# Transposing q and k by DMA instead of on TensorE for five of eight batches of an attention and mixer kernel

## The chip, the cores and the metric

The kernel runs on one core of a Trainium2 chip. The metric is the device time of one execution in microseconds (us), given as the median of several runs. One further execution was profiled; its span is the time from its first to its last instruction.

## The reference, cut to what matters

Eight batches are computed. In each, eight heads of attention over 576 positions with 64 features run under a mask: heads 0 to 3 ("plain") see the last 32 positions, heads 4 to 7 ("dilated") every fourth of the last 128. The result goes through an MLP mixer, first over tokens, then over channels.

```python
scores = scale * np.matmul(q, k.transpose(0, 1, 3, 2))      # q, k, v: (8, 8, 576, 64) float32
mask_plain = (rel >= 0) & (rel < window)                    # window 32
mask_dil = (rel >= 0) & (rel < window * dilation) & (rel % dilation == 0)   # dilation 4
...
attn = attn / (np.sum(attn, axis=-1, keepdims=True) + 1e-09)
return np.matmul(attn, v).astype(np.float32)
...
h = np.maximum(xt @ w_tok1, 0.0) @ w_tok2                   # xt: (8, 512, 576)
u = x + h.transpose(0, 2, 1)
h2 = np.maximum(u @ w_ch1, 0.0) @ w_ch2                     # 512 -> 1536 -> 512
return (u + h2).astype(np.float32)
```

## The kernel before, in words

All matrix work is float16 with float32 sums. The work is a software pipeline over the batches. In stage b (the loop at line 762) the channel MLP of batch b runs as the main thread (`gen_main`, line 517): 24 groups of four `gp` matmuls (line 529), then the `yp` matmuls (lines 546 and 566), whose sums plus `u` are stored by SyncE (SP). Steps of later batches are woven in: the attention values (`av`, line 396 and on), token mixing (`h1p`, `up`, line 438) and the transposes of the mixed rows (`tpu`, from line 467) of batch b+1, and the casts, transposes and scores of q and k of batch b+2. The loads of batch b+3 follow. Stages 1 to 5 thus hold the scores of batches 3 to 7.

The order is written out by hand: `interleave` (line 575) sorts the steps by a planned time, a number that counts about as us of TensorE work from the start of the stage, and issues each as soon as the planned time of the main thread has reached it. The scheduler is manual, so every engine executes its instructions in the order in which they are issued there, and an instruction that waits holds up everything behind it on its engine. This holds for SP too, whose only work is to issue DMAs. A DMA of SP also waits until the DMA eight places before it in this order has landed.

What happens to q and k of a batch, for each of four pairs of heads (`hp`; 0 and 1 plain, 2 and 3 dilated):

- SP loads them as float32 (`load_qk`, `load_tail`, lines 183 to 192). Partition m holds positions 4m to 4m+3, so that rows are long; the last 64 positions of both (the tails) are a tile of their own.
- GpSimd (POOL) casts them to float16 tiles `c_q`, `c_k`, `c_t` (line 103, planned from 2.0 in steps of 0.6).
- `transposes` (line 264) turns each pair around on TensorE: four 128x128 transposes for q and four for k (line 270), one for the tails (line 288 or 290), each a weight load and a matmul against the identity into PSUM. ScalarE (ACT, line 101; pairs 0 and 1) and VectorE (DVE, line 103; pairs 2 and 3) copy q from PSUM to `qz`, in two halves of 64 partitions, since the other half of each head's slot stays zero; DVE copies k to `kt` (line 275).
- `scores_plain` and `scores_dil` (lines 329 and 359) multiply `kt` and `qz` (line 320) into two PSUM banks in turn, and ACT takes the exponential into `attp` and `attd`. For batches from 2 on POOL multiplies these by the mask (line 113).

`kt` and `qz` lie in natural order of positions for the plain pairs; for the dilated pairs `qz` lies by residue of the position modulo 4, and the scores read every fourth column of `kt`. The mixed rows of batch b+1 are u = `up` + `xn`, added on DVE (line 445), one block of 128 rows after the other (s = 4, 0, 1, 2, 3); all of them are read by the `tpu` transposes.

## Time and profile before

| | |
|---|---|
| median of 3 runs | 310.79 us (310.61 to 312.88) |
| span of the profiled execution | 310.9 us, 8148 instructions |
| busy: PE, PE weight loads | 298.8 us, 268.3 us |
| busy: DVE, ACT, POOL | 168.4, 152.9, 148.4 us |
| DMA packets | 67606, 43.24 MB |
| stages 1 to 5 (from 73.00, 111.37, 145.48, 182.03 and 216.14 to 252.69 us) | 38.37, 34.11, 36.55, 34.11, 36.55 us |

The time of the profiled execution outside its span is not given apart; its span lies 0.1 us above the median of the runs, so sums made on the span carry over to the median as they are. PE is TensorE's matmuls, PEld its weight loads, which overlap with matmuls. A row of a timeline has the start in us, the duration in us, the engine, the line, the operation and its tiles (out<-in), and behind a bracket how long the engine stood idle before it and what ended that. The duration of a matmul runs from its start to its modelled end and overlaps with the next; what one costs is the distance between starts. A row of groups ends with the busy us and the mean ns of one.

### The profile page before, as it was taken

How to read it: one execution, taken by the hardware profiler on the slowest of the kernel's cores; microseconds unless marked ns; L12 is line 12 of the kernel's file. 1: busy time of each engine (PE TensorE's matmuls, PEld its weight loads, DVE VectorE, ACT ScalarE, POOL GpSimd, SP SyncE). 2: the span in 40 equal slices, each digit the busy share in tenths (PEclk: the TensorE clock that was granted, in tenths of full speed). 3: DMA queues.
4: the chain of work that ended last, by engine and by line, in shares of the span. 5: the costliest groups of instructions: out<-in, count | busy, mean ns of one | idle time of the engine just before them, and what ended most of it. 6: DMA issues, size and time to landing. Idle time of an engine off the chain costs nothing.

```text
span 310.9 us, 8148 instructions
## 1 busy us (share of the span) xinstructions
PE 298.8 (96%) x3292; PEld 268.3 (86%) x3292; DVE 168.4 (54%) x372; ACT 152.9 (49%) x349; POOL 148.4 (48%) x214
## 2 busy tenths in 40 slices
PE   5789999999999999999999999999999999999995
PEld 2677999988988999899987999899987999899884
DVE  5686448756656554655744655555745646523221
ACT  2664436286645635375545635475555635413500
POOL 7872065429970897029930897019940770000000
PEclk9999999999999999999999999999999999999999
DMA  7999999847995529821495129711001130021023
GB/s 216 267 211 180 235 268 291 242 136 215 275 293 126 170 86 289 172 70 60 121 261 136 64 92 306 153 50 57 33 2 27 45 101 3 0 70 67 2 69 103
DMA packets 67606, 43.24 MB, mean 139 GB/s; under 512 B 35920, under 2 KB 66512, under 8 KB 67568
## 3 DMA queue, kind: packets, MB, share of 16 engines
q1 hardware_dynamic: 63328, 37.63, 44.4%
q0 software_dynamic: 2640, 3.91, 7.1%
q10 hardware_dynamic: 1600, 1.18, 1.3%
q8 instruction: 26, 0.43, 0.6%
q14 instruction: 12, 0.10, 0.1%
HBM read 37.04 MB, written 9.44 MB: 149 GB/s over the span
## 4 chain that ended last, share of the span: by engine, by line
PE 91%; DVE 3%; ACT 2%; DMA 2%; issue 1%; ACTq 0%; POOLq 0%
PE gp L529 30%; PE yp L546 26%; PE h1p L426 4%; PE sc L320 4%; PE up L438 4%; PE yp L566 3%; PE tp_q L270 2%; PE tp_k L270 2%; DMA const<-consts 2%; PE sm L320 1%; PE tpu L475 1%; PE av L396 1%; PE h1p L424 1%; PE av L407 1%; PE sc L319 1%; PE tpu L467 1%
## 5 line engine op out<-in xcount | busy, mean ns | idle before, releaser
L529 PE MATMUL gp<-uT,w 128*128 128x288 f16 x768 | 109.9, 286 | 0.7 <-ACT uT L101 0.6
L546 PE MATMUL yp<-w,gt 128*128 128x256 f16 x756 | 93.8, 273 | 0.0
L107 ACT ACTIVATE gt<-gp 128x288 f16<-128x288 f32 x138 | 56.6, 410 | 72.1 <-PE gp L529 65.3
L529 PEld LDWEIGHTS <-w 128*128 128x128 f16 x768 | 83.1, 114 | 8.1 <-issue 1.2
L546 PEld LDWEIGHTS <-gt 128*128 128x128 f16 x768 | 76.0, 106 | 3.9
L113 POOL TENSOR_TENSOR attp<-attp,const 128x1280 f16<-128x1280 f16 (+1 forms) x24 | 35.8, 1515 | 77.8 <-ACT attp L349 67.0
L109 DVE TENSOR_SCALAR gt<-gp 128x288 f16<-128x288 f32 x54 | 24.6, 455 | 35.5 <-PE gp L529 33.9
L556 DVE TENSOR_TENSOR o<-yp,u 128x512 f32<-128x512 f32 x31 | 21.4, 690 | 34.4 <-PE yp L546 34.1
L113 POOL TENSOR_TENSOR attd<-attd,const 128x1024 f16<-128x1024 f16 (+1 forms) x24 | 32.8, 1394 | 0.0
L113 DVE TENSOR_TENSOR xn<-av,rec 128x320 f16<-128x320 f32 x64 | 31.5, 492 | 2.2
L320 PEld LDWEIGHTS <-kt 128*128 128x128 f16 x352 | 27.7, 104 | 3.6 <-DVE kt L275 1.4
L275 DVE COPY kt<-tp_k 128x512 f16<-128x512 f16 x32 | 21.8, 684 | 9.3 <-PE tp_k L270 9.3
L320 PE MATMUL sc<-qz,kt 128*128 128x128 f16 (+1 forms) x224 | 25.8, 228 | 1.0 <-ACT qz L101 0.7
L101 ACT COPY qz<-tp_q 64x576 f16<-64x576 f16 (+1 forms) x32 | 19.9, 621 | 6.1 <-PE tp_q L290 3.6
L340 ACT ACTIVATE attp<-sc 128x480 f16<-128x480 f32 x32 | 17.8, 573 | 9.5 <-PE sc L320 9.0
L445 DVE TENSOR_TENSOR u<-up,xn 128x512 f16<-128x512 f32 x26 | 17.9, 691 | 8.0 <-PE up L438 8.0
L103 POOL CAST c_q<-l_q 128x512 f16<-128x512 f32 x31 | 18.8, 609 | 5.7 <-DMA l_q<-in_q_dram 5.7
L369 ACT ACTIVATE attd<-sc 128x512 f16<-128x512 f32 x32 | 17.9, 596 | 5.8 <-PE sc L320 3.2
L103 POOL CAST c_k<-l_k 128x512 f16<-128x512 f32 x29 | 17.9, 619 | 4.7 <-DMA l_k<-in_k_dram 3.7
L415 DVE RECIPROCAL rec<-av 128x5 f32<-128x5 f32 x64 | 12.2, 191 | 13.2 <-PE av L402 6.9
L103 DVE COPY qz<-tp_q 64x576 f16<-64x576 f16 (+1 forms) x32 | 15.1, 471 | 7.0 <-PE tp_q L288 6.8
L101 ACT COPY uT<-tpu 128x576 f16<-128x576 f16 x15 | 9.6, 640 | 16.3 <-PE tpu L476 16.3
(123 smaller groups left out, 445.1 us busy)
## 6 DMA issues: line engine op xcount, KB each, us to landing
out_dram<-o SPq DMA_DIRECT2D x72, 128.0 KB, 2.0
l_q<-in_q_dram SPq DMA_DIRECT2D x15, 512.0 KB, 5.5
l_k<-in_k_dram SPq DMA_DIRECT2D x14, 512.0 KB, 6.5
l_vn<-in_v_dram SPq DMA_DIRECT2D x32, 128.0 KB, 6.6
l_vd<-in_v_dram SPq DMA_DIRECT2D x16, 256.0 KB, 4.3
w<-in_moe_w_ch_dram POOLq DMA_DIRECT2D x6, 512.0 KB, 7.4
lt<-in_q_dram SPq DMA_DIRECT2D x8, 128.0 KB, 3.9
l_vt<-in_v_dram SPq DMA_DIRECT2D x8, 128.0 KB, 4.8
```

What stands on the lines that cost most here:

```text
L101: nc.scalar.copy(out=out, in_=in_)
L103: eng.tensor_copy(out=out, in_=in_)
L107: nc.scalar.activation(out=out, in_=in_, func=AF.Relu)
L109: eng.tensor_scalar_max(out=out, in0=in_, scalar1=0.0)
L113: eng.tensor_tensor(out=out, in0=x, in1=y, op=ALU.mult)
L275: nc.vector.tensor_copy(out=natural(kt[hp][:, 0:512]), in_=main)
L320: nc.tensor.matmul(out=out, lhsT=kt[hp][:, keys], rhs=qz[hp][:, h, queries], start=hide is None, stop=True)
L369: nc.scalar.activation(out=a[:, h, 0:DTL], in_=p, func=AF.Exp, scale=0.125)
L445: nc.vector.tensor_tensor(out=t, in0=p, in1=xn[b][:, s], op=ALU.add)
L529: nc.tensor.matmul(out=p[:, 0:288], lhsT=w3[cb][:, 512 * (mb // 4) + mb % 4:512 * (mb // 4) + 512:4], rhs=uT[(b, cb)][:, 288 * sh:288 * sh ...
L546: nc.tensor.matmul(out=p[:, c], lhsT=gt[(b // 2, mb)][:, a0:m0 + 512:4] if half else gt[(b // 2, mb)][:, a0:a0 + 128], rhs=w4[mb][:, c], s ...
L556: nc.vector.tensor_tensor(out=o32, in0=p, in1=u16[(b, s)], op=ALU.add)
```

## The change

For batches 3 to 7 (`by_dma`) TensorE's transposes of q and k fall away. Five DMAs of SP do them, each from the float16 tiles to tiles in SBUF: one for the tails (`tt`), and for each half of the heads one for q (`qt`) and one for k (`kr`) (`dma_steps`). `place_steps` then copies from these tiles: on DVE the tails to `qz` and `kt`, the k of the plain pairs to natural order in `kt`, the q of the dilated pairs to `qz` and 128 columns of their k to `kt`; on ACT the q of the plain pairs to `qz`. The diagonal scores of the dilated pairs read `kr` as it is. The layout of `c_q` and `c_k` changes so that two pairs lie together.

The loads of batches 4 to 7 become 14 single steps, spread from 13.0 (20.0 in stage 1) in steps of 0.9, where before they were two blocks 3.0 apart. The scores of batches 3 to 7 are planned 2.2 earlier (2.0 in stage 1).

```diff
+    qta = fixed("qt", [128, 4, 4, 128])
+    kra = fixed("kr", [128, 4, 4, 128])
+    tta = fixed("tt", [128, 4, 128])
...
+    def load_steps(b):
+        def gen():
+            new_qk(b)
+            for nm in ("q", "k"):
+                load_tail(b, nm, nc.sync)
+                yield
+            for h0 in (0, 4):
+                for nm in ("q", "k"):
+                    load_qk(b, nm, h0, h0 + 4, nc.sync)
+                    yield
+            for step in load_v_steps(b):
+                step()
+                yield
+        g = gen()
+        return [lambda: next(g)] * 14
...
-            c16[(b, nm)] = sb.tile([128, 4, H, D], FP16, tag=f"c_{nm}", bufs=1, name=f"c_{nm}_{b}")
-        copy(eng, c16[(b, nm)][:, :, 2 * hp:2 * hp + 2, :],
+            c16[(b, nm)] = sb.tile([128, 4, 4, 2, D], FP16, tag=f"c_{nm}", bufs=1, name=f"c_{nm}_{b}")
+        copy(eng, c16[(b, nm)][:, hp],
...
+    def by_dma(b):
+        return b >= 3
+
+    def dma_steps(b):
+        def turn_over(t, c):
+            nc.sync.dma_start_transpose(out=t, in_=c)
+        def half(t, nm, i):
+            turn_over(t[:, 2 * i:2 * i + 2].rearrange("p a r m -> p (a r) m"),
+                      c16[(b, nm)][:, 2 * i:2 * i + 2].rearrange("m a r h d -> m (a r h d)"))
+        steps = [lambda: turn_over(tta, c16[(b, "t")].rearrange("m h d -> m (h d)"))]
+        for i in range(2):
+            for t, nm in ((qta, "q"), (kra, "k")):
+                steps.append(lambda t=t, nm=nm, i=i: half(t, nm, i))
+        return steps
+
+    def place_steps(b):
+        halves = [slice(0, 64), slice(64, 128)]
+        def tails():
+            for h in range(2):
+                nc.vector.tensor_copy(out=qza[halves[h], :, h, 512:S], in_=tta[halves[h], :, 0:64])
+            nc.vector.tensor_copy(out=kta[:, :, 512:S], in_=tta[:, :, 64:128])
+        def plain_q(hp, h):
+            nc.scalar.copy(out=natural(qz[hp][halves[h], h, 0:512]),
+                           in_=qta[halves[h], hp].rearrange("p r m -> p m r"))
+        def plain_k(hp):
+            nc.vector.tensor_copy(out=natural(kt[hp][:, 0:512]), in_=kra[:, hp].rearrange("p r m -> p m r"))
+        def dil(h):
+            nc.vector.tensor_copy(out=qza[halves[h], 2:4, h, 0:512],
+                                  in_=qta[halves[h], 2:4].rearrange("p a r m -> p a (r m)"))
+        def dil_k():
+            for hp in (2, 3):
+                nc.vector.tensor_copy(out=natural(kt[hp][:, 384:512]),
+                                      in_=kra[:, hp, :, 96:128].rearrange("p r m -> p m r"))
+        steps = [tails]
+        for hp in range(2):
+            steps.append(lambda hp=hp: plain_k(hp))
+            for h in range(2):
+                steps.append(lambda hp=hp, h=h: plain_q(hp, h))
+        for h in range(2):
+            steps.append(lambda h=h: dil(h))
+        steps.append(dil_k)
+        return steps
...
-                score(b, hp, h, p[:, 128 * r:128 * r + 128], slice(r, 512, 4),
+                score(b, hp, h, p[:, 128 * r:128 * r + 128], kra[:, hp, r] if by_dma(b) else slice(r, 512, 4),
...
-            for nm in ("q", "k"):
+            for nm in ("q", "k") if not by_dma(b) else ():
...
-            steps += score_steps(3, 24.2, 2.8) + at(9.0, 0.6, cast_steps(3))
-            steps += at(6.0, 0.0, [lambda: load_v(3)]) + at(20.0, 3.0, [lambda: emit_loads_qk(4), lambda: load_v(4)])
+            steps += score_steps(3, 22.2, 2.8) + at(9.0, 0.6, cast_steps(3))
+            steps += at(6.0, 0.0, [lambda: load_v(3)]) + at(20.0, 0.9, load_steps(4))
+            steps += at(15.0, 0.7, dma_steps(3)) + at(21.4, 0.4, place_steps(3))
...
-                steps += at(2.0, 0.6, cast_steps(b + 2)) + score_steps(b + 2, 20.6, 2.8)
+                steps += at(2.0, 0.6, cast_steps(b + 2)) + score_steps(b + 2, 18.4, 2.8)
+                steps += at(8.5, 0.7, dma_steps(b + 2)) + at(16.4, 0.5, place_steps(b + 2))
             if b + 3 < B:
-                steps += at(13.0, 3.0, [lambda b=b: emit_loads_qk(b + 3), lambda b=b: load_v(b + 3)])
+                steps += at(13.0, 0.9, load_steps(b + 3))
```

Names in the rows that follow carry the batch: `sc_5_0_1` is the score bank of batch 5, pair 0, head 1 of the pair; `u16_4_3` is u of batch 4, block 3.

On TensorE, in stage 3, the piece around the first scores of batch 5. Before:

```order
L320 MATMUL sc_5_0_0_3172<-qz_64,kt_65 128x160
...
L270 MATMUL tp_q_5_1_3177<-const_61,c_q_5_2813 128x128
...
L290 MATMUL tp_q_5_1_3177<-const_61,c_t_5_2799 128x4x32
L320 MATMUL sc_5_0_1_3186<-qz_64,kt_65 128x160
...
L270 MATMUL tp_k_5_1_3191<-const_61,c_k_5_2828 128x128
...
L546 MATMUL yp_3_0_3158<-w4_82,gt_1_0_2113 128x256
```

and now:

```order
L401 MATMUL sc_5_0_0_3076<-qz_64,kt_65 128x160
...
L401 MATMUL sc_5_0_1_3081<-qz_64,kt_65 128x160
...
L627 MATMUL yp_3_0_3087<-w4_85,gt_1_0_2074 128x256
L627 LDWEIGHTS gt_1_1_2075
```

The four transposes of q, the one of the tails and the four of k between the scores are gone, and nothing stands in their place.

On VectorE, in stage 3, from the addition that makes block 1 of u of batch 4. Before:

```order
L445 TENSOR_TENSOR u16_4_1_3048<-up_4_1_3043,xn_4_2766 128x512
L109 TENSOR_SCALAR gt_1_10_2123<-gp_3_10_1_3050 128x288
L445 TENSOR_TENSOR u16_4_2_3079<-up_4_2_3074,xn_4_2766 128x512
L445 TENSOR_TENSOR u16_4_3_3092<-up_4_3_3087,xn_4_2766 128x512
L103 COPY uT_4_0_3109<-tpu_4_0_3108 128x576
L103 COPY uT_4_1_3138<-tpu_4_1_3137 128x576
L570 TENSOR_TENSOR o32_3_4_3095<-yp_3_4_3094,u16t_1_1383 128x512
L275 COPY kt_65<-tp_k_5_0_3152 128x512
```

and now:

```order
L526 TENSOR_TENSOR u16_4_1_2969<-up_4_1_2964,xn_4_2685 128x512
L109 TENSOR_SCALAR gt_1_10_2084<-gp_3_10_1_2971 128x288
L526 TENSOR_TENSOR u16_4_2_2989<-up_4_2_2984,xn_4_2685 128x512
L354 COPY qz_64<-tt_68 64x4x64 x2
L355 COPY kt_65<-tt_68 128x4x64
L362 COPY kt_65<-kr_67 128x512
L526 TENSOR_TENSOR u16_4_3_3007<-up_4_3_3002,xn_4_2685 128x512
L362 COPY kt_65<-kr_67 128x512
L103 COPY uT_4_0_3034<-tpu_4_0_3033 128x576
L365 COPY qz_64<-qt_66 64x2x512 x2
L651 TENSOR_TENSOR o32_3_4_3013<-yp_3_4_3012,u16t_1_1386 128x512
```

Four copies from the transposed tiles stand between the additions of blocks 2 and 3 of u, where nothing stood; stages 2, 4 and 5 have the same order there, and in stage 1 the copies come behind block 3.

On SyncE, in stage 3, behind the last stores of stage 2. Before:

```order
L191 DMA lt_6_3013<-in_q_dram 64x8x64
L191 DMA lt_6_3013<-in_k_dram 64x8x64
L185 DMA l_q_6_0_3009<-in_q_dram 128x4x256
L185 DMA l_k_6_0_3011<-in_k_dram 128x4x256
L185 DMA l_q_6_1_3010<-in_q_dram 128x4x256
L185 DMA l_k_6_1_3012<-in_k_dram 128x4x256
L200 DMA l_vn_6_3056<-in_v_dram 128x4x64 x4
```

and now:

```order
L336 DMA_TRANSPOSE tt_68<-c_t_5_2718 128x4x128
L336 DMA_TRANSPOSE qt_66<-c_q_5_2732 128x8x128
L336 DMA_TRANSPOSE kr_67<-c_k_5_2747 128x8x128
L336 DMA_TRANSPOSE qt_66<-c_q_5_2732 128x8x128
L336 DMA_TRANSPOSE kr_67<-c_k_5_2747 128x8x128
L194 DMA lt_6_2937<-in_q_dram 64x8x64
L194 DMA lt_6_2937<-in_k_dram 64x8x64
L188 DMA l_q_6_0_2933<-in_q_dram 128x4x256
```

The five transposing DMAs stand ahead of the loads of batch 6, which they push back; behind, the loads of v now alternate with the stores.

More of the change, by code (lines that the diff above doesn't have):

```diff
@@ L192, in load_tail, with load_v_steps @@
                       in_=SRC[nm][b, :, 512:S, :].rearrange("h s d -> s h d"))
-    def load_v(b):
+    def load_v_steps(b):
         tn = sb.tile([128, 4, 4, D], FP32, tag="l_vn", bufs=1, name=f"l_vn_{b}")
@@ L197, in load_v, with go @@
         tx = sb.tile([128, 4, D], FP32, tag="l_vx", bufs=1, name=f"l_vx_{b}")
-        l32[(b, "vn")], l32[(b, "vd")], l32[(b, "vx")] = tn, td, tx
-        for s in range(4):
-            nc.sync.dma_start(
-                out=tn[:, s], in_=v[b, 0:4, 128 * s:128 * s + 128, :].rearrange("h s d -> s h d"))
         t = sb.tile([64, H, D], FP32, tag="l_vt", bufs=1, name=f"l_vt_{b}")
-        l32[(b, "vt")] = t
-        nc.sync.dma_start(out=t, in_=v[b, :, 512:S, :].rearrange("h s d -> s h d"))
-        for h in (0, 2):
-            nc.sync.dma_start(
-                out=td[:, h:h + 2].rearrange("m h r d -> m h (r d)"),
-                in_=v[b, 4 + h:6 + h, 0:512, :].rearrange("h (m r) d -> m h (r d)", r=4))
-        nc.sync.dma_start(out=tx, in_=v[b, 4:8, 384:512, :].rearrange("h s d -> s h d"))
+        l32[(b, "vn")], l32[(b, "vd")], l32[(b, "vx")], l32[(b, "vt")] = tn, td, tx, t
+        def go(out, in_):
+            return lambda: nc.sync.dma_start(out=out, in_=in_)
+        steps = [go(tn[:, s], v[b, 0:4, 128 * s:128 * s + 128, :].rearrange("h s d -> s h d"))
+                 for s in range(4)]
+        steps.append(go(t, v[b, :, 512:S, :].rearrange("h s d -> s h d")))
+        for h in (0, 2):
+            steps.append(go(td[:, h:h + 2].rearrange("m h r d -> m h (r d)"),
+                            v[b, 4 + h:6 + h, 0:512, :].rearrange("h (m r) d -> m h (r d)", r=4)))
+        steps.append(go(tx, v[b, 4:8, 384:512, :].rearrange("h s d -> s h d")))
+        return steps
+    def load_v(b):
+        for step in load_v_steps(b):
[10 more added lines that the diff above has]
+                    yield
+            for step in load_v_steps(b):
+                step()
+                yield
+        g = gen()
+        return [lambda: next(g)] * 14
     def emit_loads_qk(b):
@@ L319, in score @@
             nc.tensor.matmul(out=out, lhsT=ident, rhs=hide, start=True, stop=False)
-        nc.tensor.matmul(out=out, lhsT=kt[hp][:, keys], rhs=qz[hp][:, h, queries],
+        lhsT = keys if not isinstance(keys, slice) else kt[hp][:, keys]
+        nc.tensor.matmul(out=out, lhsT=lhsT, rhs=qz[hp][:, h, queries],
                          start=hide is None, stop=True)
@@ L756, in at @@
         return [(t0 + dt * i, 0.0, f) for i, f in enumerate(fs)]
-    def loads(b):
-        emit_loads_qk(b)
-        load_v(b)
     for b in range(B):
```

3 lines of the change are left out of this document (2 added, 1 removed).

## The prediction

> **What bounds the kernel now.** I read the page's busy shares and its chain of waits first, then busy time by stage, then what TensorE waited for.
>
> ```profile
> PE 298.8 (96%) x3292; PEld 268.3 (86%) x3292; DVE 168.4 (54%) x372; ACT 152.9 (49%) x349; POOL 148.4 (48%) x214
> ...
> PE 91%; DVE 3%; ACT 2%; DMA 2%; issue 1%; ACTq 0%; POOLq 0%
> ```
>
> The second row says that the chain that ended last runs over TensorE for 91% of the span. Stages 1 to 5, which the change touches, show it more sharply (us from:to, length, then busy time of PE, PEld, DVE, ACT, POOL with instructions, granted clock, DMA share, GB/s):
>
> ```profile
> 73.00:111.37 38.37, 38.26 (x440) 34.37 (x438) 22.54 (x51) 21.69 (x50) 27.55 (x34) 1.00 0.80 217
> 111.37:145.48 34.11, 34.11 (x392) 31.62 (x391) 19.60 (x44) 18.69 (x43) 18.08 (x24) 1.00 0.52 140
> 145.48:182.03 36.55, 36.55 (x405) 32.78 (x403) 20.12 (x44) 19.45 (x45) 22.43 (x28) 1.00 0.50 138
> 182.03:216.14 34.11, 34.11 (x392) 31.59 (x391) 19.59 (x44) 18.68 (x43) 17.20 (x24) 1.00 0.52 141
> 216.14:252.69 36.55, 36.55 (x404) 32.80 (x403) 20.11 (x44) 19.45 (x45) 22.45 (x28) 1.00 0.11 35
> ```
>
> In stages 2 to 5 TensorE is busy throughout at full clock, in stage 1 for all but 0.11 us; no other engine passes 72% of a stage (POOL, 27.55 of 38.37). A matmul taken out shortens such a stage by its distance to the next one, as long as what feeds TensorE keeps up.
>
> **Removed: 180 transposes.** A batch loses 36, that is per pair of heads five for q with the tails and four for k. What they cost stands in TensorE's timeline of stage 3:
>
> ```profile
> 168.82 0.38 PE L320 MATMUL sc<-qz,kt 128*128 128x160 f16 x3
> 169.04 0.39 PE L270 MATMUL tp_q<-const,c_q 128*128 128x128 f16 x4
> 169.26 0.22 PE L290 MATMUL tp_q<-const,c_t 128*128 128x128 f16 x1
> 169.32 0.37 PE L320 MATMUL sc<-qz,kt 128*128 128x160 f16 x3
> 169.53 0.39 PE L270 MATMUL tp_k<-const,c_k 128*128 128x128 f16 x4
> 169.75 1.47 PE L546 MATMUL yp<-w,gt 128*128 128x256 f16 x12
> ```
>
> The five for q go from 169.04 to 169.32, 0.28 us; the four for k from 169.53 to 169.75, 0.22 us. Four pairs make 2.0 us a batch, five batches **10.0 us**. The transposes of the next stages stand among the same neighbours, and the planned times move so that scores keep their distance to the end of the stage: they start 2.2 earlier in a stage that is 8 x 0.28 = 2.24 shorter in the plan's numbers. POOL's masks therefore keep their place too, and I cost that move at nothing.
>
> **Added: copies by DVE in front of u.** This is where I expect part of the gain back. DVE and TensorE around the end of token mixing in stage 3:
>
> ```profile
> 161.15 0.69 DVE L445 TENSOR_TENSOR u<-up,xn 128x512 f16<-128x512 f32 x1 [0.23 <-PE up L438]
> 161.76 0.45 DVE L109 TENSOR_SCALAR gt<-gp 128x288 f16<-128x288 f32 x1
> 162.56 0.69 DVE L445 TENSOR_TENSOR u<-up,xn 128x512 f16<-128x512 f32 x1 [0.36 <-PE up L438]
> 163.49 0.69 DVE L445 TENSOR_TENSOR u<-up,xn 128x512 f16<-128x512 f32 x1 [0.23 <-PE up L438]
> ...
> 163.29 1.03 PE L566 MATMUL yp<-w,gt 128*128 128x512 f16 x4
> 164.15 0.39 PE L475 MATMUL tpu<-const,u 128*128 128x128 f16 x4
> ```
>
> The last block of u is ready at 163.49 + 0.69 = 164.18, and the fourth of the `tpu` transposes, which loads it, starts some 0.17 us after 164.15: there is next to no slack. Now three copies of tails and one of k go between the additions of blocks 2 and 3. An addition occupies DVE for 0.61 us (161.15 to 161.76), so the copies begin at 162.56 + 0.61 = 163.17, and the last addition at 163.17 + P instead of 163.49, where P is their time. TensorE stands still for P - 0.32 us. No DVE copy from SBUF to SBUF in float16 is in the trace; the nearest rows are
>
> ```profile
> L275 DVE COPY kt<-tp_k 128x512 f16<-128x512 f16 x32 | 21.8, 684 | 9.3 <-PE tp_k L270 9.3
> L103 DVE COPY qz<-tp_q 64x576 f16<-64x576 f16 (+1 forms) x32 | 15.1, 471 | 7.0 <-PE tp_q L288 6.8
> L103 DVE COPY kt<-tp_q 128x64 f16<-128x64 f16 x15 | 2.9, 194 | 0.2
> L103 DVE CAST c_k<-l_k 128x512 f16<-128x512 f32 x3 | 1.6, 547 | 0.0
> ```
>
> An instruction overlaps the next by 0.08 us (0.69 against 0.61). The copy of k (512 columns) lies between 547 ns, whose source is SBUF, and 684 ns: 0.47 to 0.60 us of DVE. A copy of tails (256 columns) lies between 194 ns (64 columns) and 471 ns (576): 0.11 to 0.39. P is thus 0.80 to 1.77, and the stall 0.48 to 1.45. I take P = 1.0, nearer the low end, since the row with its source in SBUF is the shorter one: 0.68 us, in the four stages 2 to 5 **2.7 us**, with ends 1.9 and 5.8. In stage 1 the copies come behind block 3 and delay none.
>
> What else DVE and ACT get equals what they lose. DVE loses a batch's four copies of k, four of q and two of tails, 4 x 684 + 4 x 471 + 2 x 194 = 5.0 us, and gets about as many columns. ACT:
>
> ```profile
> L101 ACT COPY qz<-tp_q 64x576 f16<-64x576 f16 (+1 forms) x32 | 19.9, 621 | 6.1 <-PE tp_q L290 3.6 <-PE tp_q L270 2.2
> L101 ACT COPY uT<-tpu 128x576 f16<-128x576 f16 x15 | 9.6, 640 | 16.3 <-PE tpu L476 16.3
> L340 ACT ACTIVATE attp<-sc 128x480 f16<-128x480 f32 x32 | 17.8, 573 | 9.5 <-PE sc L320 9.0
> ```
>
> Four copies of q stay four. Only in stage 1 do all four stand in a row between two copies of uT, ahead of the first exponential: 0.64 + 4 x 0.55 + 0.64 + 0.57 = 4.1 us until the first score bank is free, where TensorE's work from there to the third group of scores, which reuses this bank, is about 3.9 us. **0.3 us**, with ends 0 and 0.6; elsewhere the pairs of copies lie apart and the `yp` matmuls cover them.
>
> **Added: 25 transposing DMAs.** When their sources are ready is POOL's business:
>
> ```profile
> 149.64 0.61 POOL L103 CAST c_t<-lt 128x512 f16<-128x512 f32 x1
> 151.31 0.61 POOL L103 CAST c_q<-l_q 128x512 f16<-128x512 f32 x1
> 151.87 0.62 POOL L103 CAST c_k<-l_k 128x512 f16<-128x512 f32 x1
> 153.54 0.62 POOL L103 CAST c_q<-l_q 128x512 f16<-128x512 f32 x1
> 154.10 0.62 POOL L103 CAST c_k<-l_k 128x512 f16<-128x512 f32 x1
> ```
>
> The first half of q can go at 151.9, of k at 152.5, the second halves at 154.2 and 154.7. Needed are tails and first half from 163.2 (DVE as above), the second half of q at about 165.9 and of k at about 168 (behind u, k, uT, two copies of q and an output addition on DVE). If each half takes S and starts only when the one before has landed, the last lands at 151.9 + 4 S: it is late from **S = 4.0 us**. No transposing DMA is in the trace. A half moves 128 x 1024 x 2 bytes = 256 KB; the nearest rows:
>
> ```profile
> l_q<-in_q_dram SPq DMA_DIRECT2D x15, 512.0 KB, 5.5
> l_vn<-in_v_dram SPq DMA_DIRECT2D x32, 128.0 KB, 6.6
> l_vd<-in_v_dram SPq DMA_DIRECT2D x16, 256.0 KB, 4.3
> ```
>
> Landing times hold a fixed part and queueing: 256 KB more cost 1.2 us (5.5 - 4.3), and DMAs in a row share the fixed 3.1. Pipelined so, four halves land by 151.9 + 3.1 + 4.8 = 159.8, over 3 us before the first need. I take 0 for them; the bounds are 0 and, wholly one after another at 5.5 us, 4 x 1.5 = 6.0 us a stage.
>
> The Trainium skill states two things on this that point apart. In "VectorE: DVE Perf Modes", section The three transpose paths, a 128x128 transpose takes 390 ns on TensorE and 1309 ns by DMA. The trace disagrees on the first: 55 ns apart here, which is what removal saves. A half is eight such blocks; by that figure, one by one, it takes an estimated 10.5 us, and the change would lose heavily. "Advanced Engine Details and Errata", section X-Bar Transpose (TRN2), gives 350 to 400 GB/s, by which a half moves in an estimated 0.75 us; no run here shows either yet.
>
> **Loads of the next batch** go behind the transposes and between the stores:
>
> ```profile
> 163.69 0.42 SPq L209 DMA_DIRECT2D l_vx<-in_v_dram  x1
> ...
> 183.59 0.60 POOL L103 CAST c_t<-lt 128x512 f16<-128x512 f32 x1
> ```
>
> The last load was issued at 163.69, and the first cast that needs one begins at 183.59: 20 us of cover hide a delay of some 5 to 12 us. Cost nothing; a store held up behind them has four output buffers.
>
> **Sum.** 310.9 - 10.0 + 2.7 + 0.3 = **303.9 us** of span; the span lay 0.1 us from the median of the runs, so this is the forecast for the median.
>
> **Rivals.**
> 1. *The copies cost nothing.* If DVE moves the four copies within 0.32 us, u is not late: 310.9 - 10.0 = 300.9. Against it: 547 ns for 512 columns, the cheapest row.
> 2. *The copies cost the most, or the DMAs are a little late*: P = 1.77 gives 310.9 - 10.0 + 5.8 + 0.6 = 307.3; S = 4.3, the row of 256 KB taken one after another, makes each stage 4 x 0.3 = 1.2 us late: 303.9 + 6.0 = 309.9. No change that can be told. For it: SP issues in order, and one queue carries all five. Against it: the loads in the trace overlap.
> 3. *Slower: the transposing DMAs become the bound.* DVE stands at the copy of the second half of k, with the output additions and the ReLUs behind it, and TensorE runs out of PSUM banks. Each us of S beyond 4.0 costs 4 us a stage, 20 in all; the 7.0 us net are gone at S = 4.35, and from 4.5 on it is over 1% slower. At the 512-KB row, S = 5.5, the time is 303.9 + 5 x 6.0 = 333.9. For it: nothing in the trace transposes by DMA, and l_vn shows 6.6 us for short rows. Against it: ten us of lead.
>
> That the transposes aren't removed is excluded by the order of the instructions.
>
> **How the numbers follow.** A measurement can tell about 1% (3.1 us). Forecast 0.60 (own range 302.8 to 307.3), no stall 0.12, about the same 0.10, slower 0.18. Faster by over 1% is 0.60 + 0.12 = 0.72, within 1% 0.10, slower 0.18. The range 300.4 to 310.5 takes in the first three cases and leaves out the slower one, whose price is open upward, and a little below.
>
> **What would show it.** Right: in stages 2 to 5 a wait of TensorE's `tpu` for u on DVE of 0.5 to 1 us each, stages 1.2 to 1.4 us shorter; halves landing within 4 us of each other's issue; no wait for them on DVE or ACT. Wrong: DVE or ACT waiting for `kr` or `qt`, or TensorE idle in the scores.

## The result and the profile after

The changed kernel takes 307.41 us (median of 4 runs, 306.74 to 308.41) against 310.87 for the kernel before, run on the same chip (4 runs, 310.61 to 312.88): a ratio of 0.9879 with an interval of 0.9839 to 0.9919. The forecast was 303.9. A gain is there, about half as large as foretold.

The page of the profiled execution (308.06 us, 1.8 us more than its span) has these rows for busy time and for the chain that ended last:

```profile
span 306.3 us, 7813 instructions
...
PE 289.6 (95%) x3112; PEld 258.5 (84%) x3112; DVE 157.3 (51%) x367; ACT 161.5 (53%) x339; POOL 148.8 (49%) x214
...
PE 86%; DVE 6%; ACT 4%; DMA 2%; issue 1%; ACTq 0%; POOLq 0%
```

TensorE has 180 matmuls less and 9.2 us less busy time, but the chain now runs over DVE and ACT for 10% of the span where it was 5%. Busy time by stage, each from its first `gp` product to that of the next (columns as before):

```profile
71.22:110.99 39.77, 37.13 (x411) 32.97 (x409) 20.86 (x51) 24.22 (x51) 28.74 (x37) 1.00 0.96 235
110.99:143.93 32.94, 32.20 (x357) 29.64 (x355) 17.43 (x42) 20.51 (x41) 18.74 (x25) 1.00 0.75 187
143.93:179.44 35.51, 34.84 (x371) 30.82 (x369) 18.11 (x43) 21.26 (x43) 22.45 (x28) 1.00 0.71 174
179.44:212.37 32.93, 32.19 (x356) 29.67 (x355) 17.43 (x42) 20.39 (x41) 17.19 (x24) 1.00 0.82 185
212.37:247.90 35.53, 34.86 (x372) 30.86 (x370) 18.11 (x43) 21.25 (x43) 22.46 (x28) 1.00 0.34 72
```

Measured between the same marks, the stages of the kernel before were 39.70, 34.12, 36.54, 34.12 and 36.54 us. Stage 1 was

```profile
71.50:111.20 39.70, 39.23 (x448) 35.11 (x445) 23.00 (x52) 22.70 (x53) 28.88 (x38) 1.00 0.79 213
```

TensorE was idle for 0.47 us there and not at all in the others; now it stands still for 0.7 us in each of stages 2 to 5 and for 2.6 in stage 1. Stages 2 to 5 are 1.18, 1.03, 1.19 and 1.01 us shorter; stage 1 is 0.07 longer. What TensorE waited for in the whole execution (us in total, times, longest):

```profile
PE tpu L556 <- DVE u L526: 3.0, 5, 0.7
...
PE sm L401 <- ACT attp L421: 2.3, 1, 2.3
```

The first wait is the forecast one: 2.6 us of it lie in stages 2 to 5, 0.4 in stage 0. Its place in stage 3, on DVE and then on TensorE:

```profile
161.17 0.69 DVE L526 TENSOR_TENSOR u<-up,xn 128x512 f16<-128x512 f32 x1 [0.36 <-PE up L519]
161.78 0.45 DVE L354 COPY qz<-tt 64x256 f16<-64x256 f16 x2
162.24 0.23 DVE L355 COPY kt<-tt 128x256 f16<-128x256 f16 x1
162.38 0.59 DVE L362 COPY kt<-kr 128x512 f16<-128x512 f16 x1
162.90 0.68 DVE L526 TENSOR_TENSOR u<-up,xn 128x512 f16<-128x512 f32 x1
```

```profile
163.64 0.23 PE L556 MATMUL tpu<-const,u 128*128 128x128 f16 x1 [0.54 <-DVE u L526]
```

From 161.78 to 162.90 the four copies take 1.12 us: P of the prediction. The bracket counts from the modelled end of the matmul before, so that a wait costs a little more in length than its idle time. The second wait, 2.3 us in one place, is in stage 1, on ACT and on TensorE:

```profile
95.03 0.64 ACT L101 COPY uT<-tpu 128x576 f16<-128x576 f16 x1 [4.21 <-PE tpu L557]
95.57 4.40 ACT L358 COPY qz<-qt 64x512 f16<-64x512 f16 x4
100.00 0.64 ACT L101 COPY uT<-tpu 128x576 f16<-128x576 f16 x1
100.53 1.04 ACT L421 ACTIVATE attp<-sc 128x480 f16<-128x480 f32 x2
```

```profile
101.16 0.36 PE L401 MATMUL sm<-qz,kt 128*128 128x160 f16 x4 [2.29 <-ACT attp L421]
```

Four copies of q in a row, 4.40 us, stand ahead of the first exponential; TensorE waits for the score bank that this exponential frees. The DMAs, issued by SP in stage 3, are in time:

```profile
148.47 1.23 SPq L336 DMA_TRANSPOSE tt<-c_t  x1
...
154.75 1.27 SPq L336 DMA_TRANSPOSE kr<-c_k  x1
```

```profile
kr<-c_k SPq DMA_TRANSPOSE x10, 3.4
```

A half lands 3.4 us after its issue (median of k; 3.3 for q), the last at about 158, and nothing reads a transposed tile before 161.78.

**How the runs below are compared.** The start of stage 1 lies between 69.56 and 71.81 us in profiled executions whose code up to there is the same, and so moves the medians by up to 2 us; the stages after it repeat to 0.02 us (the changed kernel, profiled twice, has 39.77 and 39.78, 32.94 and 32.93). In the result above, two of the four executions of the changed kernel (306.74 and 306.76 us) and three of the four of the kernel before (310.61 to 310.95) lie low, which is likely why the medians show a gain of 3.5 us and the stages 4.34; the start of an execution that was not profiled is not known. So the table gives both: the median with its ratio to the runs of the kernel before on the same chip, and the lengths of stages 1 to 5 with their sum.

| kernel | median us | ratio, interval | stages 1 to 5, us | sum |
|---|---|---|---|---|
| before | 310.87 | | 39.70, 34.12, 36.54, 34.12, 36.54 | 181.02 |
| changed | 307.41 | 0.9879 [0.9839, 0.9919] | 39.77, 32.94, 35.51, 32.93, 35.53 | 176.68 |
| e0 changed, again | 307.07 | 0.9866 [0.9836, 0.9896] | 39.78, 32.93, 35.52, 32.92, 35.52 | 176.67 |
| e1 all copies behind u | 312.11 | 1.001 [0.9982, 1.0037] | 39.79, 33.97, 36.62, 33.96, 36.63 | 180.97 |
| e2 ACT reads rows | 313.23 | 1.0057 [1.0033, 1.0082] | 43.70, 33.98, 36.57, 33.99, 36.57 | 184.81 |
| e3 q on DVE | 306.31 | 0.9845 [0.9822, 0.9868] | 38.61, 32.86, 35.22, 32.85, 35.23 | 174.77 |
| e4 loads in blocks | 306.74 | 0.9874 [0.9845, 0.9903] | 39.78, 32.94, 35.51, 32.94, 35.52 | 176.69 |
| e6 DVE copies behind u | 308.43 | 0.9904 [0.9875, 0.9934] | 39.78, 32.94, 35.54, 32.95, 35.55 | 176.76 |
| e7 DMAs twice, one place | 345.94 | (1.113 of medians) | 43.15, 43.71, 42.82, 40.40, 45.45 | 215.53 |
| e8 scores not sooner | 305.69 | 0.9826 [0.9801, 0.9852] | 37.87, 33.63, 35.26, 33.63, 35.27 | 175.66 |
| e9 e6 and e8 | 302.64 | 0.9736 [0.9706, 0.9766] | 37.86, 32.85, 34.55, 32.84, 34.55 | 172.65 |
| e10 DMAs twice, apart | 306.64 | 0.9856 [0.9831, 0.9881] | 39.77, 32.95, 35.53, 32.93, 35.52 | 176.70 |
| e11 engines swapped, gap | 302.05 | 0.9716 [0.9684, 0.9748] | 38.15, 32.07, 34.91, 32.07, 34.92 | 172.12 |
| e12 e11, tails late | 301.07 | 0.9706 [0.9672, 0.9740] | 37.36, 32.74, 34.51, 32.07, 34.52 | 171.20 |

### The profile page after: what moved, and what is told of

Its sections match the earlier page's. It is cut to its first block, busy times and chain, and to the rows that moved or that the text cites. A ratio compares the mean times of both kernels' runs of the same rounds, so it can differ in the third digit from the quotient of the medians.

```text
span 306.3 us, 7813 instructions
## 1 busy us (share of the span) xinstructions
PE 289.6 (95%) x3112; PEld 258.5 (84%) x3112; DVE 157.3 (51%) x367; ACT 161.5 (53%) x339; POOL 148.8 (49%) x214
## 3 DMA queue, kind: packets, MB, share of 16 engines
q10 hardware_dynamic: 1600, 1.18, 1.3%
## 4 chain that ended last, share of the span: by engine, by line
PE 86%; DVE 6%; ACT 4%; DMA 2%; issue 1%; ACTq 0%; POOLq 0%
PE gp L610 30%; PE yp L627 25%; PE h1p L507 5%; PE sc L401 4%; PE up L519 3%; PE yp L647 3%; DVE u L526 2%; DMA const<-consts 2%; PE sm L401 2%; ACT qz L358 1%; PE av L477 1%; PE h1p L505 1%; PE tpu L556 1%; PE av L488 1%; PE sc L399 1%
## 5 line engine op out<-in xcount | busy, mean ns | idle before, releaser
L627 PE MATMUL yp<-w,gt 128*128 128x256 f16 x756 | 94.8, 273 | 0.0
L401 PEld LDWEIGHTS <-kt 128*128 128x128 f16 x272 | 22.5, 102 | 6.0 <-issue 3.6
L358 ACT COPY qz<-qt 64x512 f16<-64x512 f16 x20 | 21.6, 1082 | 0.5
L401 PE MATMUL sc<-qz,kt 128*128 128x160 f16 (+1 forms) x144 | 18.7, 233 | 1.0 <-ACT qz L101 0.7
L107 ACT ACTIVATE h<-h1p 128x256 f16<-128x256 f32 x28 | 10.8, 384 | 10.2 <-PE h1p L507 8.3
L401 PE MATMUL sm<-qz,kt 128*128 128x64 f16 (+1 forms) x128 | 11.0, 202 | 2.5 <-ACT attp L421 2.3
```

The source lines that it names most:

```text
L107: nc.scalar.activation(out=out, in_=in_, func=AF.Relu)
L358: nc.scalar.copy(out=natural(qz[hp][halves[h], h, 0:512]), in_=qta[halves[h], hp].rearrange("p r m -> p m r"))
L401: nc.tensor.matmul(out=out, lhsT=lhsT, rhs=qz[hp][:, h, queries], start=hide is None, stop=True)
L627: nc.tensor.matmul(out=p[:, c], lhsT=gt[(b // 2, mb)][:, a0:m0 + 512:4] if half else gt[(b // 2, mb)][:, a0:a0 + 128], rhs=w4[mb][:, c], s ...
```

## The experiments

### The changed kernel again, and the copies moved behind u

e0 is the changed kernel, run beside the next three.

> The changed kernel once more, as the measure for the kernels run beside it. Theory (copies): the span is again 4 to 5 us below that of the kernel before, stage 1 as long as before (39.7 us) and stages 2 to 5 about 1.1 us shorter each; TensorE waits 2.3 us in stage 1 for a score bank and 0.5 to 0.7 us for u in each later stage. Rival (DMA traffic): where time is lost differs from run to run.

307.07 us, and the same stages to 0.02 us. In e1 all copies from the transposed tiles start later in stages 2 to 5:

```
-                steps += at(8.5, 0.7, dma_steps(b + 2)) + at(16.4, 0.5, place_steps(b + 2))
+                steps += at(8.5, 0.7, dma_steps(b + 2)) + at(17.3, 0.45, place_steps(b + 2))
```

> The copies from the transposed tiles are planned at 17.3 instead of 16.4 in stages 2 to 5, behind block 3 of u; nothing else. Theory (copies): TensorE's wait of its transposes for u (3.0 us in all, of which 0.4 in stage 0) falls to at most 0.5, and the time falls by 2 to 3 us against the changed kernel, to about 304.5 to 305. Rival (the wait only moves: DVE and ACT are late anyway, so uT or the scores wait instead): under 0.7 us gained. Rival (DMA traffic): no change.

312.11 us: the whole gain of stages 2 to 5 is gone. The waits of TensorE in e1:

```profile
PE sm L401 <- ACT attp L421: 8.8, 5, 2.3
```

The wait for u went, as it should (0.4 us are left, in stage 0), and in each of stages 2 to 5 a longer one for a score bank took its place: (8.8 - 2.3) / 4 = 1.6 us each, where the expectation for e6 below says 2.3, the length of stage 1's. This shift also moved ACT's copies of q, closer to the exponentials. So a single reason, u late on DVE, does not describe these stages. e2 and e3, run beside e1, change ACT's copies, and e6 moves DVE's alone.

### What the copies of q cost ACT

The copy on ACT was estimated at 0.55 us from a row whose source is PSUM. The groups of the changed kernel have:

```profile
L358 ACT COPY qz<-qt 64x512 f16<-64x512 f16 x20 | 21.6, 1082 | 0.5
L362 DVE COPY kt<-kr 128x512 f16<-128x512 f16 x10 | 5.9, 594 | 0.0
L365 DVE COPY qz<-qt 64x1024 f16<-64x1024 f16 x10 | 4.2, 416 | 0.2
```

ACT's row reads its 512 elements by steps of 256 bytes and writes them in a row. e2 reads them in a row and writes by steps of 8 bytes:

```
-            nc.scalar.copy(out=natural(qz[hp][halves[h], h, 0:512]),
-                           in_=qta[halves[h], hp].rearrange("p r m -> p m r"))
+            nc.scalar.copy(out=natural(qz[hp][halves[h], h, 0:512]).rearrange("p m r -> p r m"),
+                           in_=qta[halves[h], hp])
```

> ACT copies the q of the plain pairs in the order in which it lies in the transposed tile: the source is read in rows and the destination is written with a step of 8 bytes, where the changed kernel reads with a step of 256 bytes and writes in rows. Theory (the step of the read makes the copy slow): a copy takes 0.55 to 0.62 us instead of 1.08, the wait for a score bank in stage 1 falls from 2.3 to under 0.6 us, and the time by about 2 us. Rival (ACT copies float16 from SBUF at that pace in any order): 1.08 us again and no change of time.

```profile
L358 ACT COPY qz<-qt 64x512 f16<-64x512 f16 x20 | 26.9, 1345 | 0.5
```

Dearer, not cheaper; TensorE waited 7.1 us for score banks (5 times, the longest 2.8, in stage 1). Stage 1 grew by 3.9 us, of which the longer copies explain some 1.1 (4 x 0.26). The rest goes with the granted clock, which fell inside that wait (it ended at 100.87) and came back 6.8 us later:

```profile
69.88:100.00 30.12, 27.45 (x301) 23.62 (x299) 19.55 (x49) 18.56 (x37) 20.14 (x31) 1.00 0.99 217
100.00:106.82 6.82, 5.95 (x33) 4.60 (x33) 0.00 (x0) 3.02 (x7) 2.99 (x2) 0.50 1.02 278
```

5.95 us of work at half the clock cost about 3.0. This execution took 314.87 us, the longest of the ten of e2, and five of the others have a mean clock of 1.000 (311.63 to 313.25 us), so the 43.70 us of its stage 1 are not typical of e2. In stages 2 to 5 the same wait for score banks, 1.1 us each ((7.1 - 2.8) / 4), takes the gain away. e3 gives the same copies to DVE:

```
-            nc.scalar.copy(out=natural(qz[hp][halves[h], h, 0:512]),
-                           in_=qta[halves[h], hp].rearrange("p r m -> p m r"))
+            nc.vector.tensor_copy(out=natural(qz[hp][halves[h], h, 0:512]),
+                                  in_=qta[halves[h], hp].rearrange("p r m -> p m r"))
```

> DVE instead of ACT copies the q of the plain pairs; nothing else. Theory (ACT's row of four copies holds up the exponentials): a copy takes about 0.59 us on DVE, the wait for a score bank in stage 1 falls from 2.3 us to under 0.3, and the time by about 2 us; the waits for u stay at 0.5 to 0.7 us. Rival (DVE becomes late): uT and the output additions on DVE come up to 2 us later a stage and TensorE waits for a score or an output bank instead, no gain or a loss of 1 to 2 us.

```profile
L358 DVE COPY qz<-qt 64x512 f16<-64x512 f16 x20 | 11.9, 596 | 0.3
```

```profile
PE tpu L556 <- DVE u L526: 3.0, 5, 0.7
...
PE sm L401 <- DVE kt L370: 1.1, 1, 1.1
```

DVE needs 0.60 us for what takes ACT 1.08. The waits for ACT's exponentials are gone; stage 1 is only 1.2 us shorter, since TensorE now waits 1.1 there for DVE's last copy of keys, which comes behind the four copies and beside POOL's masks:

```profile
98.26 3.17 DVE L365 COPY qz<-qt 64x1024 f16<-64x1024 f16 x2
...
101.95 2.45 DVE L370 COPY kt<-kr 128x128 f16<-128x128 f16 x1
```

```profile
98.35 6.35 POOL L113 TENSOR_TENSOR attp<-attp,const 128x1280 f16<-128x1280 f16 x4 [8.38 <-ACT attp L430]
```

The first row is 0.86 us in the changed kernel, the second 0.45 for two: copies on DVE that took far longer while POOL worked. They come up again in e11. In stages 2 to 5 the wait for u stays, and 0.1 to 0.3 us a stage are won.

### Only DVE's copies behind u; the scores not sooner; both

e6 moves DVE's copies of pairs 0 and 1 alone behind the fourth block of u and leaves ACT's where the change has them:

```
-                steps += at(8.5, 0.7, dma_steps(b + 2)) + at(16.4, 0.5, place_steps(b + 2))
+                steps += at(8.5, 0.7, dma_steps(b + 2))
+                late = (17.3, 17.4, 17.4, 17.9, 17.5, 18.9, 19.4, 19.9, 20.4, 20.9)
+                steps += [(t, 0.0, f) for t, f in zip(late, place_steps(b + 2))]
```

> The changed kernel with only the DVE copies of hp 0 and 1 (the three tails, the two copies kt<-kr) put behind u of the fourth block in stages 2 to 5; ACT's copies of q stay where the change has them. The earlier shift of all copies behind u took the wait of the transposes of u away and gave a wait of 2.3 us for a score bank in each of these stages instead. Theory (that new wait came from ACT's four copies of q, 1.08 us each, which had moved too): here the transposes of u wait only in stage 0 (0.4 us in all), the wait sm<-ACT attp stays at the 2.3 us of stage 1 alone, and the time is 2.0 to 2.6 us below the changed kernel's 307.1, that is 304.5 to 305.1. Rival (the scores sooner have no slack at all, so whatever delays kt is waited for): sc or sm waits for DVE kt by 0.6 us or more in stages 2 to 5, and the time stays within 0.7 us of 307.1.

308.43 us, and every stage within 0.03 us of the changed kernel's. Both theory and rival missed how: no later wait for keys came, but TensorE's waits have

```profile
PE sm L401 <- ACT attp L421: 5.5, 5, 2.3
```

and ACT in stage 3 stands as it stood, in e6 and, below, in the changed kernel:

```profile
162.14 2.19 ACT L358 COPY qz<-qt 64x512 f16<-64x512 f16 x2
...
167.78 1.04 ACT L421 ACTIVATE attp<-sc 128x480 f16<-128x480 f32 x2
```

```profile
162.10 2.18 ACT L358 COPY qz<-qt 64x512 f16<-64x512 f16 x2
...
167.71 1.04 ACT L421 ACTIVATE attp<-sc 128x480 f16<-128x480 f32 x2
```

ACT works without a break from 162.1 into its exponentials in both. TensorE waits for these in e6, in stage 3,

```profile
168.41 0.36 PE L401 MATMUL sm<-qz,kt 128*128 128x160 f16 x4 [0.87 <-ACT attp L421]
```

where in the changed kernel the same matmul, at 168.34, stood idle for 0.13 us and the one for u for 0.54. Once TensorE no longer stopped for u it came earlier to the score bank by about as much and waited there instead. Two chains end together in stages 2 to 5: removing the one for u alone wins nothing.

e8 undoes the sooner scores alone:

```
-            steps += score_steps(3, 22.2, 2.8) + at(9.0, 0.6, cast_steps(3))
+            steps += score_steps(3, 24.2, 2.8) + at(9.0, 0.6, cast_steps(3))
...
-                steps += at(2.0, 0.6, cast_steps(b + 2)) + score_steps(b + 2, 18.4, 2.8)
+                steps += at(2.0, 0.6, cast_steps(b + 2)) + score_steps(b + 2, 20.6, 2.8)
```

> The changed kernel with the scores at their old places in the order (24.2 in stage 1, 20.6 in stages 2 to 5; the change has 22.2 and 18.4). Theory (in stage 1 ACT's four copies of q, 4.4 us in a row, hold up the first exponentials, and the rest of the stage has slack): the score banks' wait for ACT falls from 2.3 us to under 0.5, the transposes of u still wait 0.7 us in stages 2 to 5, and the time is 1.5 to 2.3 us below 307.1, that is 304.8 to 305.6. Rival (the scores have to come sooner, since the stage has lost 2 us of matmuls ahead of them and the last exponentials would reach into the next stage): the next stage's first products wait for the last exponentials by 0.4 us or more a stage, and the time is 307.5 to 310.

305.69 us, the edge of what the theory gave. Stage 1 falls by 1.9 us to 37.87, and the wait sm for ACT attp is 0.4 us instead of 2.3.

Stages 3 and 5 are 0.26 us shorter each, and stages 2 and 4 are 0.7 longer each. TensorE's idle time in these two grew by 0.4 each, in two waits for dilated exponentials (0.31 and 0.10) of the kind that the rival named; the rest is not assigned. So the sooner scores cost stage 1 its gain and were worth 0.7 us in stages 2 and 4; in sum they cost 1.0 us. e9 does both shifts:

> The changed kernel with both shifts: the DVE copies of hp 0 and 1 behind u of the fourth block (stages 2 to 5), and the scores at their old places. Each alone took one wait away: the first left every stage's length as it was (32.94, 35.54, 32.95, 35.55 us), since a wait for ACT's exponentials of 0.8 us a stage took the place of the wait for u; the second shortened stage 1 from 39.78 to 37.87, and left the wait for u. Theory (two waits that cover each other in stages 2 to 5, u on DVE and the copies of q on ACT): with both gone, neither shows by more than 0.4 us a stage, stage 1 stays at 37.9, stages 2 to 5 lose another 0.5 to 0.7 us each against the second shift alone (33.63, 35.26, 33.63, 35.27), and the time is 303.0 to 304.0 against its 305.7. Rival (a third wait stands behind them, such as sc for DVE kt or the last exponentials, or the next stage's start): stages 2 to 5 stay within 0.2 us of 33.63 and 35.26, and the time is 305.2 or more.

302.64 us, slightly better than the theory's range. TensorE waits for u in stage 0 alone, and for score banks 1.2 us in stages 1 to 5 (0.35 in stage 1, 0.41 each in stages 2 and 4). Against e8, stages 2 to 5 are 0.78, 0.71, 0.79 and 0.72 us shorter, which is what the wait for u cost once ACT was out of its way.

### Loads in blocks

e4 issues the loads in two blocks, as before the change:

```
-                steps += at(13.0, 0.9, load_steps(b + 3))
+                steps += at(13.0, 3.0, [lambda b=b: emit_loads_qk(b + 3), lambda b=b: load_v(b + 3)])
```

> The changed kernel with the loads issued as before, in two blocks (6 at one place, 8 at another), instead of as 14 single steps. Theory (the loads are hidden both ways; in the changed kernel they are done over 20 us before their casts): 307.1 within 0.7 us, and no new wait of a cast. Rival (a block of loads holds SP's queue, whose issues take 0.4 to 0.6 us each, so that the transposing DMAs or the stores behind it come late): the DVE copies wait for kr or qt, or the output tiles for their stores, by 1 us or more a stage, and the time is 309 or more.

306.74 us and the changed kernel's stages to 0.02 us: the spread of the loads does nothing here, either way.

### The transposing DMAs doubled

e7 issues each transposing DMA twice to the same place:

```
-            nc.sync.dma_start_transpose(out=t, in_=c)
+            for _ in range(2):
+                nc.sync.dma_start_transpose(out=t, in_=c)
```

> The changed kernel with every transposing DMA issued twice in a row, to the same place. Theory (the transposing DMAs are hidden): the first issue in stage 3 was at 148.5 us and each took SP 1.27 us, so that five more move the last landing from 158 to about 164.4 us, the first pair's k to about 159.5; its copy starts at 162.4 and the second pair's q is copied at 164.7, so that the time stays at 307.1, within 1 us, and no DVE or ACT copy waits for kr or qt by more than 0.3 us. Rival (they hold the queue or the memory that others need): stages 1 to 5 grow by about 1.27 us for each of the five, up to 6 us a stage, and the time is above 311.

345.94 us. The theory failed by its own premise, that two issues take SP 2 x 1.27 us. The second must not start before the first has landed, so SP's queue waits, as its rows in stage 3 show:

```profile
169.52 4.29 SPq L337 DMA_TRANSPOSE qt<-c_q  x2
173.90 4.36 SPq L337 DMA_TRANSPOSE kr<-c_k  x2
```

```profile
180.28 0.59 DVE L363 COPY kt<-kr 128x512 f16<-128x512 f16 x1 [5.10 <-DMA kr<-c_k]
180.79 0.68 DVE L527 TENSOR_TENSOR u<-up,xn 128x512 f16<-128x512 f32 x1
```

A pair takes 4.3 us instead of 1.3 for one. DVE stands 5.10 us at the copy of k with the addition of u behind it, and TensorE waits for u:

```profile
PE tpu L557 <- DVE u L527: 26.4, 5, 9.2
```

Stage 3 grew by 7.3 us, of which TensorE's idle time is 5.1; its granted clock was 0.92 there, which goes with the rest. That is close to the prediction's third rival, but at the first copy of k instead of that of the second half, and brought about by the wait of each pair. e10 writes the first of each two into a tile that nothing reads, so that neither waits, and plans the ten in steps of 0.35 instead of 0.7:

```
+        steps = [lambda t=t: turn_over(t, c16[(b, "t")].rearrange("m h d -> m (h d)")) for t in (ttb, tta)]
...
+            for t, nm in ((qtb, "q"), (qta, "q"), (krb, "k"), (kra, "k")):
```

> The changed kernel with every transposing DMA done twice, the first time into a tile that nothing reads, so that the second need not wait for the first to land as it did when both wrote one place (4.3 us for a pair, against 1.27 for one issue, and 8.4 us of waits of DVE for kr). Theory (the DMAs overlap, and SP's issue of 1.27 us sets their pace): ten take 12.7 us from 148.5 in stage 3, the last lands at about 164.5, the first pair's k at about 159, and the second pair's k is copied at 167; the stages stay within 0.3 us of 39.78, 32.94, 35.54 and the time within 1 us of 307.1. Rival (their transfers share something of 3 us each and do not overlap): ten take 30 us, the first pair's k lands at about 166 and is waited for by 3 us or more in stages 2 to 5, and the time is 320 or more.

306.64 us, the stages unchanged to 0.02 us. SP in stage 3:

```profile
153.87 1.29 SPq L339 DMA_TRANSPOSE krb<-c_k  x1
...
157.95 1.33 SPq L339 DMA_TRANSPOSE qt<-c_q  x1
```

One issue every 1.36 us (153.87 to 157.95 for three), each landing in 3.3 to 3.4 us (median of the groups): they overlap. Twice the transposing traffic is still hidden.

### Engines swapped, and copies in DVE's gap

e11 gives DVE the four copies of q that go by steps and ACT the two that lie in a row, and puts the tails, the first k and the first two copies of q where DVE waited 2.6 us for TensorE, ahead of `gt` of block 8:

```
+                when = (12.0, 12.1, 12.2, 12.3, 17.3, 17.4, 17.5, 17.6, 17.7, 19.9)
+                steps += [(t, 0.0, f) for t, f in zip(when, place_steps(b + 2))]
```

> The changed kernel with the copies of q swapped between the engines: DVE does the four that put queries back into order (64x512 each, read by steps of 256 bytes), ACT the two of hp 2 and 3 that copy 64x1024 as they lie; and in stages 2 to 5 the tails, the first k and the first two q copies come before gt of block 8, where DVE now waits 2.6 us for PE, and the others behind u of the fourth block. Theory of the waits: ACT has 2.2 us less to do if its plain copy takes 0.55 us for 512 elements (the step is what makes it take 1.08), u and the exponentials are both on time, stage 1 is 38.6 or less, stages 2 to 5 are 32.2 to 32.5 and 34.6 to 34.9, and the time is 302.5 to 304.5. Rival on the price (ACT takes as long for f16 from SBUF however it lies): its 64x1024 copy takes 2.1 us, the two of them 4.2 us, ACT's wait in stage 1 stays near 2.3 us and the time is near 307. Rival on the gap (k lands too late for a copy at that place and holds gt up behind it): DVE waits for kr in stages 2 to 5, and the time is 307 or more.

302.05 us. Its groups have

```profile
L358 DVE COPY qz<-qt 64x512 f16<-64x512 f16 x20 | 12.0, 598 | 0.2
L365 ACT COPY qz<-qt 64x1024 f16<-64x1024 f16 x10 | 10.4, 1044 | 0.2
```

On ACT 1024 elements in a row take 1.04 us, as long as 512 by steps of 256 bytes. So the order of access, and not SBUF as the source, is what doubled the price. "ScalarE: Activation LUTs" of the Trainium skill, section What ACT_TABLE_LOAD costs, gives an ACTIVATE without pointer operands 186 ns and 0.833 per element; taken for a copy that is an estimated 1039 ns for 1024, which the trace matches (1044), and 613 for 512, which it does not where the read goes by steps (1082). "SBUF — State Buffer", section Door 1: The DMA port swizzle, says that accesses need at least two hits in a line of 16 bytes for full rate; a step of 256 bytes has one, which fits the row, but a step of 8 bytes has two, and took 1345 ns in e2.

Stages 2 and 4 are as short as the sum of the removed transposes allows (34.12 - 2.0 = 32.1). Stages 3 and 5 are not, and DVE and POOL show why:

```profile
152.32 2.29 DVE L354 COPY qz<-tt 64x256 f16<-64x256 f16 x2
154.63 0.23 DVE L355 COPY kt<-tt 128x256 f16<-128x256 f16 x1
```

```profile
152.22 0.61 POOL L103 CAST vv<-l_vt 64x512 f16<-64x512 f32 x1
...
153.90 0.40 POOL L103 CAST vt<-l_vx 128x256 f16<-128x256 f32 x1
```

Two copies that take 0.45 us elsewhere took 2.29 and ended 0.3 us after POOL's last cast; TensorE waited 0.23 us for the `gt` behind them. e12 moves the tails behind u, and the scores of stage 1 back:

```
-                when = (12.0, 12.1, 12.2, 12.3, 17.3, 17.4, 17.5, 17.6, 17.7, 19.9)
+                when = (17.3, 12.1, 12.2, 12.3, 17.4, 17.4, 17.5, 17.6, 17.7, 19.9)
```

> The kernel with the copies of q swapped between the engines, with two more shifts: the tails (L354, L355) go behind u of the fourth block, and the scores of stage 1 to their old place (24.2). In the run before, the two copies qz<-tt took 2.29 us in stage 3 (152.3 to 154.6, 0.45 us where POOL sat idle) while POOL was casting, gt of block 8 came late behind them, and the odd stages were 34.91 us. Theory (a DVE copy of f16 that lies in a row waits until POOL is done; away from POOL's casts it takes 0.22 us): the copies qz<-tt take 0.25 us each or less in all stages, gp waits for DVE gt by 0.1 us or less, stages 3 and 5 fall to 34.5 or 34.6, stages 2 and 4 stay at 32.1, stage 1 falls from 38.15 to 37.9 or less, and the time is 300.8 to 301.6. Rival (whatever copy stands first in that place is held up, POOL's casts or a late k being the limit of the place): the copy kt<-kr there ends as late as before, 155.3 us in a stage that began at 141.94, gp waits for gt by 0.2 us still, the odd stages stay at 34.9, and the time is 301.6 to 302.2.

301.07 us, the fastest. The copies of tails take 216 ns again, stages 3 and 5 fall to 34.5 and stage 1 to 37.36. Stage 2 speaks for the rival: at 32.74 it is 0.67 us longer than in e11. DVE there, and in stage 3:

```profile
119.81 0.98 DVE L362 COPY kt<-kr 128x512 f16<-128x512 f16 x1 [2.17 <-DMA kr<-c_k]
```

```profile
151.56 1.11 DVE L362 COPY kt<-kr 128x512 f16<-128x512 f16 x1 [1.28 <-DMA kr<-c_k]
```

The copy of k now stands first, waits for its DMA, and takes 0.98 and 1.11 us instead of 0.60 beside POOL's casts, which end at 120.33 and 152.21; it ends 0.46 us after each. This copy reads by steps, so that the theory's "in a row" is not the condition. TensorE waits 0.5 us for `gt` in stage 2. Of the ten us that the transposes took, e12 keeps 181.02 - 171.20 = 9.8.

## Why the prediction was partly right

- **The transposes: right.** 10.0 us were to go, and with the waits mended 9.8 go.
- **u behind DVE's copies: right in place and size, wrong as the only price.** P was taken as 1.0 and is 1.12, for which the prediction's P - 0.32 gives 0.80 us a stage; the waits in stages 2 to 5 are 2.6 us in all against 2.7, and cost 0.71 to 0.79 a stage from e8 to e9. But e6 shows that without them nothing is won, since ACT's copies end at the same time. "Elsewhere the pairs of copies lie apart and the `yp` matmuls cover them" was wrong: in stage 3 ACT works from 162.10 to 168.75 with one copy of uT between the pairs. The sum counted one chain where two ran side by side.
- **The step that failed: the copies of q on ACT in stage 1.** They were priced at 0.55 us each, from a row that reads PSUM, with 0.3 us of wait and an end of 0.6. They took 1.08, four of them 4.40 where 2.2 were reckoned, and the wait was 2.3. "Four copies of q stay four" was true of the count and not of the duration. e3 and e8, by two different ways, take the wait away and shorten stage 1 by 1.2 and 1.9 us.
- **The sooner scores, costed at nothing: wrong.** POOL's masks do keep their place (in stage 3 they begin 10.1 us before its end, where it was 9.6), but ACT's copies stand ahead of the exponentials, and 2 us of lead would have hidden them in stage 1: 1.9 us there, 1.0 in the sum of the stages (e8).
- **The DMAs hidden, the loads free: right.** A half lands in 3.3 us, below the S of 4.0 at which it would have been late even one after another; in truth they overlap, one every 1.36 us (e10), which is 193 GB/s at the pace of SP's issues. The figure of 1309 ns a block in "VectorE: DVE Perf Modes" of the Trainium skill, section The three transpose paths, would have made an estimated 10.5 us of each half; the trace has 3.3 us for eight blocks, landing included. DMA share rose, and neither DVE nor ACT waits for `kr` or `qt` in the changed kernel.
- **Span and median.** The span was said to carry over to the median as it is. An execution takes 1.8 us more than its span (308.06 against 306.3), so the span of 310.9 before belonged to an execution slower than the median. The sum's 7.0 us of gain should be set against the stages: 4.34 measured.

The bookkeeping of stages 1 to 5: of the 10.0 us removed, stage 1 kept none of its 2.0 and grew by 0.07; the chain of u and that of ACT behind it cost 3.0 in stages 2 to 5 (e8 to e9), and ACT's another 0.5 in stages 3 and 5 (0.26 each, what e8 wins there). That leaves 4.4; 4.34 came. TensorE idle in the scores, which the prediction gave as a sign of being wrong, was there: 2.3 us in stage 1, 0.13 in stage 3. The direction, faster by over 1%, came true by little (1.2%), and 307.41 lies just above the forecast's own 302.8 to 307.3. Of the rivals, the first (copies that cost nothing, 300.9) is the time that e12 reaches with both chains mended (301.07), the second is near in time (307.3) by luck, as neither of its two causes was at work, and the third takes a wait for each DMA, as e7 has.

## What to carry to other kernels

When work moves from one engine's path to others, price the moved copies by their access pattern and not by their count: a copy of the same size took 0.60, 1.08 or 1.35 us by engine and step. A wait that is removed alone may win nothing, because another engine ends at the same moment; look at both engines' rows ahead of the same matmul and mend them together. Compare stages between fixed marks where the start of an execution scatters by more than the effect.

## What was not expected of the hardware

- ACT copies float16 from SBUF to SBUF at 1.04 us for 1024 elements in a row, 1.08 for 512 read by steps of 256 bytes and 1.35 for 512 written by steps of 8. DVE takes 0.42 for the first and 0.60 for the second.
- DVE's float16 copies were held up while POOL worked: 3.17 us for 0.86 (e3), 2.29 for 0.45 (e11), 0.98, 1.11 and, in stage 5, 2.02 for 0.60 (e12). In the 13 traces with DMA transposes, DVE makes 625 copies from `tt`, `qt` and `kr`. 19 of them started while POOL was at work on a cast or a mask; all 19 were held, and each ended as if it had begun 0.13 to 0.14 us before the end of a POOL instruction and then taken its usual time. The five that began just ahead of a POOL instruction were not held. "SBUF — State Buffer", section Who interferes with whom, of the Trainium skill says that the two share a pair of ports under an exclusive lock when such a copy runs in a two-port mode; the rows agree, though none shows the mode.
- A transposing DMA of 256 KB mostly occupies SP for 1.23 to 1.29 us to issue (three of the changed kernel's twenty took 1.42 to 2.48), against 0.4 to 0.65 for a load, and lands in 3.3 to 3.4 us; a second one to the same place waits for that (4.3 us for a pair).
- In e2 the granted clock fell to 0.50 inside TensorE's 2.8 us stall of stage 1 and was 1.00 again after 6.8 us; around the 2.3 us stall of the profiled execution of the changed kernel it stayed at 1.00. What decides between them stays open: five of e2's ten executions have a mean clock of 1.000, and one of the changed kernel's, which was not profiled, has 0.994.
